# Immediate cosine constants, small temporaries in one PSUM tile, and wider row statistics in an S4D convolution with a SwiGLU block

## The chip, the cores and the metric

The kernel runs on one core of a Trainium2 chip. The metric is the time of one execution on the device, in microseconds. Its engines are named as the profile names them: PE (TensorE matmul), PEld (its weight load), DVE (VectorE), ACT (ScalarE), POOL (GpSimd) and SP (SyncE, which issues the DMAs).

## The reference

The input `x` has L = 2048 positions of D = 640 channels. The block normalises each position, modulates it by a condition, convolves each channel along the positions with a kernel made from N = 128 complex modes, and then does a gated feed-forward part of width 1728.

```python
def _A_ref(u, log_A_real, A_imag, C_real, C_imag, log_dt, D_skip):
    dt = jnp.exp(log_dt)
    A = -jnp.exp(log_A_real) + 1j * A_imag
    C = (C_real + 1j * C_imag) * dt[:, None]
    P = jnp.exp((A * dt[:, None])[:, :, None] * pos[None, None, :])
    K = 2.0 * jnp.einsum("dn,dnl->dl", C, P).real
    y = irfft(rfft(u^T, 2L) * rfft(K, 2L))[:, :, :L]^T      # causal convolution
    return y + u * D_skip
mod = (silu(c) @ w_mod).reshape(1, 6, 1, -1)                # sa, ca, ga, sb, cb, gb
h = layernorm(x) * (1 + ca) + sa
x = x + ga * _A_ref(h, ...)
h = layernorm(x) * (1 + cb) + sb
x = x + gb * ((silu(h @ w1) * (h @ w3)) @ w2)
```

(The transforms are written in shorthand here.)

## The kernel before

**Two parts.** The first part makes the condition's modulation, the row statistics of the first normalisation, the convolution kernels and the convolution. The second is the feed-forward part (FFN), a long run of matmuls. The first part is a plan of named tasks. A task has an engine, the tasks it comes after, and slots that it takes and gives back. The table `ORDER` lists all tasks by number in the order in which they are issued; `Plan.sequence` (L175) reads it. Every engine then works strictly in that order: the wrapper `InOrder` (L150) chains each instruction behind the one before it on its engine, and this is why nearly every instruction of the profile carries the line L150. From the last task on a scheduler orders the FFN.

**Generation.** The kernels K are made for five blocks of 128 channels, in eight chunks of 16 channels each, 40 chunks in all (`gen_chunk`, L523; `gen_tasks`, L1676). Per chunk POOL adds phases (`ph`) and multiplies sizes (`xx`, `yy`, `x`), ACT takes an absolute value of the phases and four sines `tr` of 128x512, two of them as sines and two as cosines (sine of pi/2 minus the phase, L559), DVE multiplies them into `xx` and `yy`, PE sums the modes by 64 small matmuls into the product `kps` of 128x256, and ACT copies `kps` into `ks`. The product has one PSUM bank to itself (tag "kg", one buffer). The cosine takes pi/2 from `hpi`, a column of 128 values in SBUF that POOL fills in `setup`.

**The first row statistics.** The positions lie in four row blocks `xs` of 128 rows by 4 by 640. For three blocks, ACT makes a sum (a Copy with an accumulator output, into `h_nm`), DVE turns the four sums of a block into minus the mean, and ACT makes the sum of squares about the mean (a Square with `h_nm` as its bias, accumulator into `h_ss`) (`h_stats`, L338). For the fourth block, DVE does both with `bn_stats` over two halves of 320 channels and `bn_aggr` into `h_mv`, and then writes its columns of `h_nm` and `h_ss` (`end`, L360). A chain of small DVE steps (`rsqrt`, L242) makes the inverse root for all 16 columns from `h_ss`; in this call two of its temporaries (`rsw`) already lie in PSUM. The normalised rows `hn` are then made by ACT and DVE. The modulation matmuls are `pm`, their copy is `m`, the rows spread from it are `prow`.

**The second statistics.** The last inverse transform leaves its results on PE row by row (`iy`), DVE adds each to the rows `x2` (x for the first, late for the second group of four) and takes statistics of the sum by `bn_stats` over 128 channels each, four of them as the first 512 channels are done and the fifth after the last 128 channels (`iyb`) are added. `bn_aggr` makes mean and variance in `mv`. The FFN does the same for two later row groups (`ln_stats`, L627).

Of the kernel before, what the change touches and what calls it, by code (L numbers as in the profile page):

```python
# [18 lines left out]
P = 128  # L19
L = 2048  # L20
D = 640
# [59 lines left out]
1399 1395 1388 1450 1396 1400 1447 1389 1397 1398 1401 1390 1452 1392 1409 1402 1465 1393 1449 1411 1410 1391 1403 1414 1412 1416  # L81
1454 1415 1413 1417 1404 1451 1418 1419 1407 1405' 1459 1408 1460 1406 1479 1422 1420 1487 1423 1480 1461 1421 1467 1475 1482 1453
# [3 lines left out]
1578 1502 1547 1548 1512 1549 1543 1579 1550 1551 1554' 1553 1580 1555' 1509 1513 1552' 1510 1556 1581 1560 1511 1582 1587 1643 1564  # L86
# [5 lines left out]
"""  # L92
# [112 lines left out]
class K:  # L205
# [18 lines left out]
    def setup(self):  # L224
        nc = self.nc
        c = self.const = self.pool("const")
        self.ident = c.tile([P, P], F32, name="ident")
        make_identity(nc, self.ident)
        self.hpi = c.tile([P, 1], F32, name="hpi")
        nc.gpsimd.memset(self.hpi, HPI)  # L230
        self.ones = c.tile([P, 1], F32, name="ones")
        nc.gpsimd.memset(self.ones, 1.0)
        self.cols = c.tile([P, 3, KT], F32, name="cols")
        c.tile([P, 32], F32, name="pad")
        d = self.dram = self.pool("dram", space=DRAM)
        self.hs = d.tile([NB, 4, 4, 32, 4, P], F32, name="hs")
        self.zd = d.tile([32, 2, 64, D], F32, name="zd")
        self.w2d = d.tile([14, P, 2, D], F32, name="w2d")
        self.xv = self.x.rearrange("(t1 q j) d -> q t1 j d", t1=32, q=4, j=NJ)
        self.ov = self.out.rearrange("(t1 q j) d -> q t1 j d", t1=32, q=4, j=NJ)  # L240

    def rsqrt(self, pool, var, n, tag, mean, scale=1.0, work=None):  # L242

        nc = self.nc
        v, w = (pool.tile([P, n], F32, name=f"rs_{x}_{tag}", tag=f"rs_{x}") for x in "vw")
        y = pool.tile([P, n], F32, name=f"rs_y_{tag}", tag="rs_y", bufs=2)
        nb = pool.tile([P, n], F32, name=f"rs_n_{tag}", tag="rs_n", bufs=2)
        t, u = work or (pool.tile([P, n], F32, name=f"rs_t_{tag}", tag="rs_t"), w)
        nc.vector.tensor_scalar(v, var, scale, EPS, op0=ALU.mult, op1=ALU.add)
        wi = w.bitcast(I32)  # L250
        nc.vector.tensor_scalar(wi, v.bitcast(I32), 1, None, op0=ALU.logical_shift_right)
        nc.vector.tensor_scalar(wi, wi, -1.0, float(0x5F3759DF), op0=ALU.mult, op1=ALU.add)
        for i in range(3):

            if work:
                nc.vector.tensor_copy(u, w)
            nc.vector.tensor_mul(t, u, w)
            nc.vector.scalar_tensor_tensor(t, t, -0.5, v, op0=ALU.mult, op1=ALU.mult)
            nc.vector.scalar_tensor_tensor(y if i == 2 else w, t, 1.5, w, op0=ALU.add, op1=ALU.mult)
        m, s = mean  # L260
        nc.vector.scalar_tensor_tensor(nb, m, s, y, op0=ALU.mult, op1=ALU.mult)
        return y, nb

    def ln_begin(self, pool, tag):
        return (pool.tile([P, 4, KT, 6], F32, name=f"st_{tag}", tag="ln_st", bufs=2),
                pool.tile([P, 4, 2], F32, name=f"mv_{tag}", tag="ln_mv", bufs=2))

    def ln_part(self, st, xs, j, c0, c1):
        for c in range(c0, c1):
            self.nc.vector.bn_stats(st[:, j, c, :], xs[:, j, c * P:(c + 1) * P])  # L270

# [29 lines left out]
    def load_c(self, e):  # L301
        nc = self.nc
        ct = e.tile([P, KT], F32, name="ct")
        nc.sync.dma_start(ct, self.c.rearrange("o (k p) -> p (o k)", p=P))
        th = e.tile([P, KT], F32, name="th")
        self.sc = self.const.tile([P, KT], F32, name="sc")

        def sc():
            nc.vector.scalar_tensor_tensor(self.sc, th, 1.0, ct, op0=ALU.add, op1=ALU.mult)
            nc.vector.tensor_scalar(self.sc, self.sc, 0.5, None, op0=ALU.mult)  # L310
        return lambda: nc.scalar.activation(th, ct, AF.Tanh, scale=0.5), sc
# [26 lines left out]
    def h_stats(self, xs, b):  # L338
# [3 lines left out]
        def sums(j):  # L342
            nc.scalar.activation(xs[:, j], xs[:, j], AF.Copy, accum_out=self.h_nm[:, 4 * b + j:4 * b + j + 1])

        def mean():
            o = slice(4 * b, 4 * b + 4)
            nc.vector.tensor_scalar(self.h_nm[:, o], self.h_nm[:, o], -1.0 / D, None, op0=ALU.mult)

# [3 lines left out]
        if b in self.W["stat_v"]:  # L352
            st = self.gp.tile([P, 4, 2, 6], F32, name=f"h_st{b}", tag="h_st", bufs=1)
            mv = self.gp.tile([P, 4, 2], F32, name=f"h_mv{b}", tag="h_mv", bufs=1)

# [167 lines left out]
    def gen_chunk(self, d0, tabs, off, E, place):  # L523
# [27 lines left out]
        def sines(i):  # L551
# [74 lines left out]

    def ln_stats(self, b, st, mv, c0):  # L627
        for j in range(4):
            self.ln_part(st, self.x2[b], j, c0, KT)
        return self.ln_end(self.fp, st, mv, f"n{b % 2}")  # L630
# [376 lines left out]
    def tail_tasks(self, border, cut):  # L1007
# [109 lines left out]
        def rows(b, rank):  # L1117
            for j in range(4 * b, 4 * b + 4):
# [40 lines left out]
        def last_stats(b):  # L1159
            for j in range(4):  # L1160
                self.ln_part(self.stats[b][0], self.x2[b], j, KT - 1, KT)
        add("izb0", "SP", 0, lambda: last_load(0), ends, -100, dma=[131072] * 4, take=[("w2", 1)])
# [7 lines left out]
        def prepare(b, rank):  # L1170
# [8 lines left out]
            add(f"lm{b}", "DVE", .68, mean, [f"isb{b}"] + [f"is{j}.{c}" for j in range(4 * b, 4 * b + 4) for c in range(2)], rank)  # L1179
            if b == 0:  # L1180
# [177 lines left out]
    def groups(self, p, tiles, X, acc, W, w2, pend):  # L1358

        for m in tiles:  # L1360
# [24 lines left out]
            if p == 0 and m in (8, 10):  # L1385
                b = m // 2 - 2
                self.stats[b % 2] = self.ln_stats(b, *self.ln_begin(self.fp, f"n{b}"), 0)
        return pend
# [95 lines left out]
    def run(self):  # L1484
# [118 lines left out]
    def param_steps(self, T, bs):  # L1603
# [23 lines left out]
             ("arc", lambda V: (A.activation(at, k, AF.Arctan), A.activation(s, at, AF.Sin),  # L1627
                                A.activation(m, at, AF.Sin, scale=-1.0, bias=self.hpi)))],
            [tt(k, k, s, ALU.mult),
# [46 lines left out]
    def gen_tasks(self, b):  # L1676
# [266 lines left out]
    def early_tasks(self, e):  # L1943
# [175 lines left out]
```

## Time and profile before

| | |
|---|---|
| time, median of three runs | 955.36 us (954.37 to 956.51) |
| the profiled execution | 954.89 us |
| its span in the profile | 953.1 us |
| PE busy | 870.5 us (91%) |
| DVE busy | 682.3 us (72%) |
| ACT busy | 551.5 us (58%) |
| POOL busy | 344.1 us (36%) |

The table's shares are means over the whole span. The views used below are: the busy time of each engine in chosen stretches, the groups of equal instructions (busy time, mean length, idle time in front of them and what ended it), the waits of one engine in a stretch, and the timeline of one engine, where each row has its start, its length, and in brackets the idle time before it and the engine and result that ended it. A row with "x4" holds four instructions of a kind in a row, and its length goes from the start of the first to the end of the last.

### The profile page before, as it was taken

What the parts mean: (1) busy time and instruction counts of PE and PEld (TensorE: products, weight loads), DVE (VectorE), ACT (ScalarE), POOL (GpSimd) and SP (SyncE); (2) the same over time, 40 slices, a digit from 0 to 9 for tenths busy, and PEclk for the clock granted to TensorE, in tenths of its full rate; (3) what the DMA queues carried; (4) which work ended last, traced back from release to release, by engine and by line L of the source; (5) the groups of instructions that cost most, each with busy time, mean ns of one, the idle gap of its engine ahead of it and who ended that gap; (6) DMA issues with size and microseconds to landing.
All of it is one profiled execution on the core that took longest, in us unless ns stands there. A gap on an engine that the chain in (4) does not pass through costs nothing.

```text
span 953.1 us, 21244 instructions
## 1 busy us (share of the span) xinstructions
PE 870.5 (91%) x8369; PEld 689.6 (72%) x8369; DVE 682.3 (72%) x1290; ACT 551.5 (58%) x1036; POOL 344.1 (36%) x376
## 2 busy tenths in 40 slices
PE   1266999999989997899999999999999999999997
PEld 1134968877878875686777778888788888888775
DVE  7988999999989878776676775657555555555412
ACT  3989999998877733644444444545444444443312
POOL 2698999999987400011111111000121212120000
PEclk9987999999999997999999999999999999999999
DMA  9974454453173578754444412375432222221374
GB/s 199 284 266 112 158 134 137 101 146 83 47 173 93 134 189 212 179 179 125 148 116 123 139 63 91 92 237 168 130 91 84 83 84 83 84 84 38 110 217 132
DMA packets 110508, 127.42 MB, mean 134 GB/s; under 512 B 10568, under 2 KB 90696, under 8 KB 109128
## 3 DMA queue, kind: packets, MB, share of 16 engines
q1 hardware_dynamic: 110120, 125.80, 46.9%
q8 instruction: 66, 1.08, 0.5%
q14 instruction: 34, 0.28, 0.1%
q10 hardware_dynamic: 288, 0.26, 0.1%
HBM read 95.89 MB, written 30.15 MB: 132 GB/s over the span
## 4 chain that ended last, share of the span: by engine, by line
PE 55%; DMA 2%; ACT 2%; DVE 2%; SPq 1%; issue 1%; DVEq 0%
PE c L150 19%; PE acc L150 18%; PE X L150 12%; PE gu L150 3%; PE iy L150 1%; DMA w2r<-in_w 1%; DMA w<-w2d 1%; PE to L150 1%; PE tp L150 1%; PE gh L150 1%; ACT oc L978 0%; PE iyb L150 0%; SPq L991 0%; DMA izb<-zd 0%; DMA zd<-zt 0%
## 5 line engine op out<-in xcount | busy, mean ns | idle before, releaser
L150 PE MATMUL acc<-ah,w 128*128 128x512 f32 x560 | 173.0, 394 | 3.0 <-DMA w<-w2d 2.3
L150 PEld LDWEIGHTS acc<-ah,w 128*128 128x128 f32 x560 | 103.7, 188 | 26.6 <-issue 2.7
L775 POOL TENSOR_TENSOR s<-wr 128x256 f32<-128x256 f32 x22 | 16.6, 753 | 277.3 <-DMA wr<-in_w 133.0
L150 PE MATMUL acc<-al,w 128*128 128x512 f32 x260 | 102.2, 393 | 0.0
L599 DVE TENSOR_TENSOR wl<-s,wh 128x256 fp32r<-128x256 f32 x92 | 39.0, 424 | 67.3 <-ACT wh L598 66.8
L598 ACT ACTIVATE wh<-s 128x256 fp32r<-128x256 f32 x92 | 37.6, 410 | 78.3 <-PE X L150 57.9
L150 POOL TENSOR_TENSOR ph<-p,p 128x1024 int32<-128x1024 int32 x40 | 79.0, 1974 | 6.4 <-ACT tr L150 4.2
L598 ACT ACTIVATE wh<-wr 128x256 fp32r<-128x256 f32 x92 | 38.4, 418 | 57.6 <-PE X L150 42.0
L776 POOL TENSOR_TENSOR s<-s,wr 128x256 f32<-128x256 f32 x22 | 16.6, 753 | 132.2 <-issue 130.9
L150 DVE TENSOR_TENSOR yy<-yy,tr 128x512 f32<-128x512 f32 (+1 forms) x60 | 56.8, 947 | 6.3 <-POOL yy L150 3.3
L150 PE MATMUL kps<-yy,xx 128*32 128x64 f32 x1920 | 38.2, 230 | 22.4 <-DVE xx L150 19.9
L150 ACT ACTIVATE tr<-ph,hpi 128x512 f32<-128x512 f32 x80 | 54.4, 689 | 6.9 <-DVE yy L150 5.9
L836 ACT ACTIVATE t<-g 128x512 f32<-128x512 f32 x44 | 27.8, 632 | 52.7 <-DVE g L800 52.7
L150 PEld LDWEIGHTS acc<-al,w 128*128 128x128 f32 x260 | 48.9, 188 | 10.8 <-DVE al L599 0.4
L805 DVE SCALAR_TENSOR_TENSOR g<-t,g 128x512 f32<-128x512 f32 x48 | 33.7, 702 | 31.2 <-ACT t L836 29.3
L150 PEld LDWEIGHTS kps<-yy,xx 128*32 128x32 f32 x1920 | 32.7, 114 | 31.1 <-issue 17.5
L150 DVE TENSOR_TENSOR xx<-tr,xx 128x512 f32<-128x512 f32 x80 | 54.3, 683 | 0.7
L150 PE MATMUL fz<-fp,wz 64*128 64x512 f32 x224 | 54.5, 607 | 0.1
L599 DVE TENSOR_TENSOR wl<-wr,wh 128x256 fp32r<-128x256 f32 x92 | 40.7, 443 | 14.8 <-ACT wh L598 14.7
L150 ACT ACTIVATE tr<-ph 128x512 f32<-128x512 int32 x80 | 46.5, 598 | 4.2 <-DVE yy L150 2.7
L150 PE MATMUL ps<-wk,xb 128*64 128x128 f32 x640 | 46.8, 294 | 1.2 <-DVE hb L150 0.4
L598 ACT ACTIVATE ah<-h 128x512 fp32r<-128x512 f32 x26 | 16.5, 633 | 53.8 <-PE acc L150 53.8
(452 smaller groups left out, 2450.7 us busy)
## 6 DMA issues: line engine op xcount, KB each, us to landing
w<-w2d SPq DMA_DIRECT2D x42, 640.0 KB, 3.9
wr<-in_w SPq DMA_DIRECT2D x50, 320.0 KB, 3.6
zd<-zt SPq DMA_DIRECT2D x40, 256.0 KB, 2.5
w2d<-w SPq DMA_DIRECT2D x14, 640.0 KB, 3.5
xs<-in_x SPq DMA_DIRECT2D x16, 320.0 KB, 10.9
hs<-hb SPq DMA_DIRECT2D x20, 256.0 KB, 2.8
xb<-hs SPq DMA_DIRECT2D x20, 256.0 KB, 5.5
iz<-zd SPq DMA_DIRECT2D x32, 160.0 KB, 4.3
```

Of the source, the lines that this page charges most:

```text
L150: self.prev = self.k.order(f(*a, **kw), self.prev)
L598: self.nc.scalar.activation(H, v, AF.Copy)
L599: eng.tensor_tensor(Lo, v, H.bitcast(F32), op=ALU.subtract)
L775: eng.tensor_tensor(s[0], u[:, 0:2], u[:, 2:4], op=ALU.add)
L776: eng.tensor_tensor(s[1], s[0], g[:, 0:2], op=ALU.subtract)
L805: V.scalar_tensor_tensor(g, th, 1.0, g, op0=ALU.add, op1=ALU.mult)
L836: tanh = lambda o, i: A.activation(o, i, AF.Tanh, scale=0.5)
```

## The change

Three edits. The order table's numbers shift, since two statistics tasks per row become one; the tasks keep their order, except that these merged tasks of the second row group stand further ahead (third place below).

1. Cosines take pi/2 as an immediate of the instruction; the column `hpi` goes.
2. A PSUM tile `small` of 128x512 stays in the bank that the product had. Its second half is `kps` of every chunk. Its first half holds the silu's temporaries (columns 0 to 12), the sums and the sums of squares of the first statistics (`h_sum`, `h_ss`, columns 16 to 47) and the fourth block's means and variances. `h_nm` stays in SBUF. `rsqrt` writes its first shift to another of its temporaries.
3. `bn_stats` of the second statistics runs over 512 and 128 channels, not five times 128.

```diff
-        self.hpi = c.tile([P, 1], F32, name="hpi")
-        nc.gpsimd.memset(self.hpi, HPI)
...
-                A.activation(t, ab[:, :, 4 - i, :], AF.Sin, scale=-SINS, bias=self.hpi)
+                A.activation(t, ab[:, :, 4 - i, :], AF.Sin, scale=-SINS, bias=HPI)
...
+        self.small = psg.tile([P, 512], F32, name="small", tag="kg", bufs=1)
...
-                kps[c] = self.psg.tile([P, 256], F32, name=f"kps{b}{c}", tag="kg", bufs=1)
+                kps[c] = self.small[:, 256:]
...
-        th = e.tile([P, KT], F32, name="th")
+        th, u = self.small[:, :KT], self.small[:, 8:8 + KT]
...
-        for x in ("h_nm", "h_ss"):
-            setattr(self, x, self.gp.tile([P, NJ], F32, name=x))
+        self.h_nm = self.gp.tile([P, NJ], F32, name="h_nm")
+        self.h_sum, self.h_ss = self.small[:, 16:32], self.small[:, 32:48]
...
-            nc.scalar.activation(xs[:, j], xs[:, j], AF.Copy, accum_out=self.h_nm[:, 4 * b + j:4 * b + j + 1])
+            nc.scalar.activation(xs[:, j], xs[:, j], AF.Copy, accum_out=self.h_sum[:, 4 * b + j:4 * b + j + 1])
...
-            nc.vector.tensor_scalar(self.h_nm[:, o], self.h_nm[:, o], -1.0 / D, None, op0=ALU.mult)
+            nc.vector.tensor_scalar(self.h_nm[:, o], self.h_sum[:, o], -1.0 / D, None, op0=ALU.mult)
...
-            mv = self.gp.tile([P, 4, 2], F32, name=f"h_mv{b}", tag="h_mv", bufs=1)
+            mv = self.small[:, 64 + 8 * b:72 + 8 * b].rearrange("p (j a) -> p j a", a=2)
...
-        nc.vector.tensor_scalar(wi, v.bitcast(I32), 1, None, op0=ALU.logical_shift_right)
-        nc.vector.tensor_scalar(wi, wi, -1.0, float(0x5F3759DF), op0=ALU.mult, op1=ALU.add)
+        ui = u.bitcast(I32)
+        nc.vector.tensor_scalar(ui, v.bitcast(I32), 1, None, op0=ALU.logical_shift_right)
+        nc.vector.tensor_scalar(wi, ui, -1.0, float(0x5F3759DF), op0=ALU.mult, op1=ALU.add)
...
-    def ln_part(self, st, xs, j, c0, c1):
-        for c in range(c0, c1):
-            self.nc.vector.bn_stats(st[:, j, c, :], xs[:, j, c * P:(c + 1) * P])
+    def ln_part(self, st, xs, j, c):
+        self.nc.vector.bn_stats(st[:, j, c, :], xs[:, j, 512 * c:min(512 * c + 512, D)])
...
-                for c in range(2):
-                    add(f"is{j}.{c}", "DVE", .4, lambda j=j, c=c: self.ln_part(self.stats[b][0], self.x2[b], j % 4, 2 * c, 2 * c + 2), [f"ia{j}"], rank + .1)
+                add(f"is{j}", "DVE", .6, lambda j=j: self.ln_part(self.stats[b][0], self.x2[b], j % 4, 0), [f"ia{j}"], rank + .1)
```

What stands where is seen best in the program's order. First ACT in the startup, where the sums (`xs` with `h_nm` as second output, Copy) and the squares (`xs` with `h_ss`) of three row blocks stand among the first sines. Before:

```order
L150 ACTIVATE tr0_0_338<-ph_0_313 128x512 [waits Pool_49]
L150 ACTIVATE xs0_185,h_nm_134<-xs0_185 128x640
L150 ACTIVATE xs1_148,h_ss_135<-xs1_148,h_nm_134 128x640 [waits DVE_49]
L150 ACTIVATE xs0_185,h_nm_134<-xs0_185 128x640
L150 ACTIVATE xs1_148,h_ss_135<-xs1_148,h_nm_134 128x640
L150 ACTIVATE xs2_176,h_ss_135<-xs2_176,h_nm_134 128x640 [waits DVE_49]
L150 ACTIVATE tr1_0_363<-ph_0_313 128x512
```

The same place after the change; `small` is the PSUM tile:

```order
L150 ACTIVATE tr0_0_334<-ph_0_309 128x512 [waits Pool_49]
L150 ACTIVATE xs0_182,small_78<-xs0_182 128x640 [waits DVE_49,Activation_49]
L150 ACTIVATE xs1_145,small_78<-xs1_145,h_nm_133 128x640 [waits Activation_49]
L150 ACTIVATE xs0_182,small_78<-xs0_182 128x640 [waits Activation_49]
L150 ACTIVATE xs1_145,small_78<-xs1_145,h_nm_133 128x640 [waits Activation_49]
L150 ACTIVATE xs2_173,small_78<-xs2_173,h_nm_133 128x640 [waits DVE_49]
L150 ACTIVATE tr1_0_359<-ph_0_309 128x512
```

The order is the same. Each statistic now waits for the one before it on ACT, and the first of these rows also waits for DVE, which reads `small` ahead of it.

Second, DVE in the startup, where the fourth block's statistics are put together (`h_st` are its partial statistics) and PE's first product follows on them. Before, and after:

```order
L150 BN_AGGR h_mv_236<-h_st_235 128x2 x2
L150 BN_AGGR h_mv_236<-h_st_235 128x2 [waits DVE_49]
L150 BN_AGGR h_mv_236<-h_st_235 128x2
L150 TENSOR_SCALAR h_nm<-h_mv_236 128x4 [waits DVE_49]
L150 TENSOR_SCALAR h_ss<-h_mv_236 128x4
L150 SCALAR_TENSOR_TENSOR yy_373<-yy_373,tr_16_456 128x16x32 [waits Activation_49,Pool_49]
```

```order
L150 BN_AGGR small<-h_st_232 128x2 [waits Activation_49]
L150 BN_AGGR small<-h_st_232 128x2 [waits DVE_49] x3
L150 TENSOR_SCALAR h_nm<-small 128x4 [waits DVE_49]
L150 TENSOR_SCALAR small<-small 128x4 [waits DVE_49]
L150 SCALAR_TENSOR_TENSOR yy_369<-yy_369,tr_16_451 128x16x32 [waits Activation_49,Pool_49]
```

Again nothing moved, and the first aggregate waits for ACT's last statistic ahead of it, the other five for the one before. PE's first product, `kps<-yy,xx` before and `small<-yy,xx` now, waited for DVE's `xx` and for POOL; now it waits for the last of these rows and for ACT as well. The next statistic on ACT waits for the end of that product.

Third, DVE at the end of the first part, where the rows of the last inverse transform (`iy`, then `iyb`) are added and their statistics taken (`st`). Before:

```order
L150 TENSOR_TENSOR x_94<-iy_5338,x_94 128x512 [waits PE_49]
L150 BN_STATS st_5020<-x_94 128x6 x2
L150 TENSOR_TENSOR late<-iy_5344,late 128x512 [waits PE_49]
L150 BN_STATS st_5020<-x_94 128x6 [waits DVE_49]
L150 BN_STATS st_5020<-x_94 128x6 x3
L150 TENSOR_TENSOR late<-iy_5357,late 128x512 [waits PE_49]
L150 TENSOR_TENSOR late<-iy_5361,late 128x512 [waits PE_49]
L150 BN_STATS st_5020<-x_94 128x6 x4
L150 TENSOR_TENSOR x_94<-iyb_5395,x_94 128x4x128 [waits PE_49]
```

After:

```order
L150 TENSOR_TENSOR x_93<-iy_5295,x_93 128x512 [waits PE_49]
L150 BN_STATS st_4976<-x_93 128x6 [waits DVE_49]
L150 TENSOR_TENSOR late<-iy_5300,late 128x512 [waits PE_49]
L150 BN_STATS st_4978<-late 128x6 [waits DVE_49]
L150 TENSOR_TENSOR late<-iy_5310,late 128x512 [waits PE_49]
L150 BN_STATS st_4978<-late 128x6 [waits DVE_49]
L150 TENSOR_TENSOR late<-iy_5315,late 128x512 [waits PE_49]
L150 BN_STATS st_4978<-late 128x6 [waits DVE_49]
L150 TENSOR_TENSOR x_93<-iyb_5343,x_93 128x4x128 [waits PE_49]
```

The statistics of the second row group (`late`), which stood behind the `iyb` addition, now stand ahead of it, one behind each addition: eight of 512 channels where sixteen of 128 were.

More of the change, by code (lines that the diff above doesn't have):

```diff
@@ L81 @@
 1399 1395 1388 1450 1396 1400 1447 1389 1397 1398 1401 1390 1452 1392 1409 1402 1465 1393 1449 1411 1410 1391 1403 1414 1412 1416
-1454 1415 1413 1417 1404 1451 1418 1419 1407 1405' 1459 1408 1460 1406 1479 1422 1420 1487 1423 1480 1461 1421 1467 1475 1482 1453
[3 rows of a table removed]
-1578 1502 1547 1548 1512 1549 1543 1579 1550 1551 1554' 1553 1580 1555' 1509 1513 1552' 1510 1556 1581 1560 1511 1582 1587 1643 1564
[5 rows of a table removed]
+1454 1415 1413 1417 1404 1451 1418 1419 1407 1405' 1459 1408 1460 1406 1477 1422 1420 1483 1423 1478 1479 1461 1421 1467 1474 1453
[3 rows of a table added]
+1542 1543 1546' 1545 1572 1547' 1501 1505 1544' 1502 1548 1573 1552 1503 1574 1579 1635 1556 1575 1598 1560 1549 1633 1580 1564 1550
[5 rows of a table added]
 """
@@ L233, in setup @@
         self.cols = c.tile([P, 3, KT], F32, name="cols")
-        c.tile([P, 32], F32, name="pad")
+        c.tile([P, 40], F32, name="pad")
         d = self.dram = self.pool("dram", space=DRAM)
@@ L264, in ln_begin @@
     def ln_begin(self, pool, tag):
-        return (pool.tile([P, 4, KT, 6], F32, name=f"st_{tag}", tag="ln_st", bufs=2),
+        return (pool.tile([P, 4, 2, 6], F32, name=f"st_{tag}", tag="ln_st", bufs=2),
                 pool.tile([P, 4, 2], F32, name=f"mv_{tag}", tag="ln_mv", bufs=2))
-    def ln_part(self, st, xs, j, c0, c1):
-        for c in range(c0, c1):
-            self.nc.vector.bn_stats(st[:, j, c, :], xs[:, j, c * P:(c + 1) * P])
+    def ln_part(self, st, xs, j, c):
+        self.nc.vector.bn_stats(st[:, j, c, :], xs[:, j, 512 * c:min(512 * c + 512, D)])
     def ln_mean(self, st, mv):
@@ L304, in load_c @@
         nc.sync.dma_start(ct, self.c.rearrange("o (k p) -> p (o k)", p=P))
-        th = e.tile([P, KT], F32, name="th")
+        th, u = self.small[:, :KT], self.small[:, 8:8 + KT]
         self.sc = self.const.tile([P, KT], F32, name="sc")
         def sc():
-            nc.vector.scalar_tensor_tensor(self.sc, th, 1.0, ct, op0=ALU.add, op1=ALU.mult)
-            nc.vector.tensor_scalar(self.sc, self.sc, 0.5, None, op0=ALU.mult)
+            nc.vector.scalar_tensor_tensor(u, th, 1.0, ct, op0=ALU.add, op1=ALU.mult)
+            nc.vector.tensor_scalar(self.sc, u, 0.5, None, op0=ALU.mult)
         return lambda: nc.scalar.activation(th, ct, AF.Tanh, scale=0.5), sc
@@ L625, in inverse_row, with ln_stats @@
         return half
-    def ln_stats(self, b, st, mv, c0):
+    def ln_stats(self, b, st, mv):
         for j in range(4):
-            self.ln_part(st, self.x2[b], j, c0, KT)
+            for c in range(2):
+                self.ln_part(st, self.x2[b], j, c)
         return self.ln_end(self.fp, st, mv, f"n{b % 2}")
@@ L1160, in last_stats @@
             for j in range(4):
-                self.ln_part(self.stats[b][0], self.x2[b], j, KT - 1, KT)
+                self.ln_part(self.stats[b][0], self.x2[b], j, 1)
         add("izb0", "SP", 0, lambda: last_load(0), ends, -100, dma=[131072] * 4, take=[("w2", 1)])
@@ L1178, in mean @@
                 ln[b], steps[0] = self.ln_steps(self.fp, self.stats[b][1], f"n{b}")
-            add(f"lm{b}", "DVE", .68, mean, [f"isb{b}"] + [f"is{j}.{c}" for j in range(4 * b, 4 * b + 4) for c in range(2)], rank)
+            add(f"lm{b}", "DVE", .68, mean, [f"isb{b}"] + [f"is{j}" for j in range(4 * b, 4 * b + 4)], rank)
             if b == 0:
@@ L1386, in groups @@
                 b = m // 2 - 2
-                self.stats[b % 2] = self.ln_stats(b, *self.ln_begin(self.fp, f"n{b}"), 0)
+                self.stats[b % 2] = self.ln_stats(b, *self.ln_begin(self.fp, f"n{b}"))
         return pend
@@ L1627, in param_steps @@
              ("arc", lambda V: (A.activation(at, k, AF.Arctan), A.activation(s, at, AF.Sin),
-                                A.activation(m, at, AF.Sin, scale=-1.0, bias=self.hpi)))],
+                                A.activation(m, at, AF.Sin, scale=-1.0, bias=HPI)))],
             [tt(k, k, s, ALU.mult),
```

16 rows, old and new, of the table ORDER are left out of this document.

## The prediction

> **What bounds the kernel now.** I read the profiled execution (954.89 us, span 953.1 us) first in stretches of time, since an average over a kernel with a generation part and a matmul part says little. Columns: busy microseconds of PE, PEld, DVE, ACT and POOL, then the granted clock.
>
> ```profile
> 60.00:80.00 20.00, 7.59 (x214) 5.14 (x217) 16.29 (x36) 17.63 (x34) 17.30 (x20) 0.83 0.49 169
> 80.00:100.00 20.00, 17.94 (x405) 13.04 (x397) 17.82 (x31) 17.96 (x30) 18.93 (x18) 0.91 0.67 169
> 100.00:150.00 50.00, 48.49 (x1000) 39.09 (x1000) 48.69 (x71) 48.67 (x89) 47.32 (x49) 1.00 0.50 136
> 150.00:200.00 50.00, 48.35 (x1020) 40.78 (x1019) 48.88 (x75) 48.76 (x86) 48.89 (x49) 1.00 0.44 114
> 200.00:250.00 50.00, 49.62 (x1026) 39.60 (x1024) 48.68 (x76) 45.47 (x77) 48.18 (x46) 1.00 0.38 99
> 250.00:300.00 50.00, 47.59 (x1020) 40.01 (x1018) 44.08 (x74) 36.77 (x63) 44.42 (x47) 0.97 0.42 105
> 300.00:350.00 50.00, 50.00 (x974) 42.01 (x970) 43.01 (x75) 32.02 (x59) 17.78 (x15) 1.00 0.65 157
> 500.00:600.00 100.00, 100.00 (x439) 77.12 (x438) 67.24 (x150) 45.36 (x94) 15.12 (x20) 1.00 0.32 99
> ```
>
> Three different regimes. Up to 80 us PE is nearly empty and the other engines hand work round in a fixed order. From 100 to 250 us four engines are each about 97% busy, so none of them is the bound alone. From 300 us, and in the whole FFN, PE is full. An edit to DVE or ACT in the FFN is therefore worth nothing; one in the startup moves everything behind it; one in the middle is worth only what the other three engines let through.
>
> **The cosines.** The cosine read a column `hpi` as its bias, the sine has none. From the costliest groups, then DVE's waits from 100 to 250 us:
>
> ```profile
> L150 ACT ACTIVATE tr<-ph,hpi 128x512 f32<-128x512 f32 x80 | 54.4, 689 | 6.9 <-DVE yy L150 5.9
> L150 ACT ACTIVATE tr<-ph 128x512 f32<-128x512 int32 x80 | 46.5, 598 | 4.2 <-DVE yy L150 2.7
> ```
>
> ```profile
> DVE x L150 <- ACT tr L150: 0.9, 2, 0.5
> DVE yy L150 <- ACT tr L150: 0.5, 1, 0.5
> ```
>
> With an immediate the cosine should take the sine's 598 ns: 80 x 0.091 = 7.3 us of ACT work goes. How much of it reaches the end? DVE, busy for 146.25 of the 150 us, waited for ACT only 0.9 + 0.5 = 1.4 us there; when ACT hands over sooner, these waits go and DVE's own work is next. I take 1.4 us off the end. The bounds are 0 (ACT's time turns into waits for DVE, which are already the cosines' releaser in the row) and the full 7.3: PE's idle time from 80 to 300 us is 2.06 + 1.51 + 1.65 + 0.38 + 2.41 = 8.0 us, so PE would allow it.
>
> **Small temporaries in one PSUM tile.** `small` is one tile in one bank, and in the built program its users wait for one another although their columns are disjoint (the listings above show it): the accumulator outputs on ACT, the aggregates on DVE, and the product of each generation chunk on PE. ACT's timeline first (start, duration, instruction, idle before):
>
> ```profile
> 31.36 0.19 ACT L150 ACTIVATION_READ_ACCUMULATOR xs<-xs 128x1 f32 x1
> 31.46 0.72 ACT L150 ACTIVATE xs<-xs 128x640 f32<-128x640 f32 x1
> ...
> 38.63 0.72 ACT L150 ACTIVATE xs<-xs 128x640 f32<-128x640 f32 x1
> ...
> 39.95 0.83 ACT L150 ACTIVATE xs<-xs,h_nm 128x640 f32<-128x640 f32 x1 [0.50 <-DVE h_nm L150]
> ...
> 42.31 0.81 ACT L150 ACTIVATE xs<-xs,h_nm 128x640 f32<-128x640 f32 x1
> ...
> 50.68 0.81 ACT L150 ACTIVATE xs<-xs,h_nm 128x640 f32<-128x640 f32 x1
> ...
> 52.53 0.81 ACT L150 ACTIVATE xs<-xs,h_nm 128x640 f32<-128x640 f32 x1
> ...
> 56.23 0.67 ACT L150 ACTIVATE tr<-ph,hpi 128x512 f32<-128x512 f32 x1
> 57.41 0.65 ACT L150 ACTIVATE m<-pm 128x384 f32<-128x384 f32 x2 [0.50 <-PE pm L150]
> ...
> 70.70 1.95 ACT L150 ACTIVATE hn<-sp,rs_n_h,rs_y_h 128x128 f32<-128x128 f32 x4 [0.67 <-ACT ph L150]
> ...
> 73.06 3.80 ACT L150 ACTIVATE hn<-sp,rs_n_h,rs_y_h 128x128 f32<-128x128 f32 x8
> ```
>
> A statistic is an ACTIVATE and a read of its accumulator; the next ACTIVATE starts at 31.46, 0.09 before that read ends (31.36 + 0.19). When it must wait for the read, the 0.09 goes, and a wait on the engine itself costs a little more: 0.02 to 0.04 in the `hn` rows, taking 0.46 us as one's length ((3.80 - 0.46) / 7 = 0.477 from start to start). That is 0.12 per adjacent pair.
>
> DVE's timeline of the same stretch:
>
> ```profile
> 38.74 0.87 DVE L150 BATCH_NORM_STATS2 h_st<-xs 128x6 f32<-128x320 f32 x2
> ...
> 41.62 0.33 DVE L150 TENSOR_SCALAR h_nm<-h_nm 128x4 f32<-128x4 f32 x1 [1.64 <-ACT xs L150]
> ...
> 50.52 0.41 DVE L150 BATCH_NORM_AGGREGATE h_mv<-h_st 128x2 f32<-128x12 f32 x4
> 50.97 0.94 DVE L150 TENSOR_SCALAR h_nm<-h_mv 128x4 f32<-128x4 f32 x1
> 51.82 1.11 DVE L150 TENSOR_SCALAR h_ss<-h_mv 128x4 f32<-128x4 f32 x1
> ...
> 66.60 0.52 DVE L150 TENSOR_SCALAR rs_v_h<-h_ss 128x16 f32<-128x16 f32 x1
> 67.16 0.17 DVE L150 TENSOR_SCALAR rs_w_h<-rs_v_h 128x16 int32<-128x16 int32 x1
> ```
>
> Then PE's, and one row of POOL's:
>
> ```profile
> 50.75 1.96 PE L150 MATMUL kps<-yy,xx 128*32 128x64 f32 x64 [7.65 <-DVE xx L150]
> 52.64 0.29 PE L150 MATMUL kps<-dsk,ident 32*32 32x4 f32 x8
> ...
> 66.23 1.16 PE L150 MATMUL kps<-x,xx 128*32 128x64 f32 x64 [1.25 <-DVE xx L150]
> ```
>
> ```profile
> 58.12 1.95 POOL L150 TENSOR_TENSOR ph<-p,p 128x1024 int32<-128x1024 int32 x1
> ```
>
> The replay, step by step:
>
> 1. The Copy at 38.63 now waits for the two `h_nm` on DVE that read `small` and end at about 40.0: +1.35. The 0.50 of waiting behind it is used up, so the first Square is at +0.9. The third `h_nm` (41.62) now waits for the Square that stands behind the sum it needs, and the Square of 42.31 waits for it: about 43.9, +1.6.
> 2. Four adjacent Squares up to 50.68 add 4 x 0.12 = 0.5, two cosines give 0.2 back: the last Square before the aggregates ends at 51.58 + 2.0 = about 53.5.
> 3. The first aggregate (50.52) now waits for that Square, and the six small DVE instructions wait each for the last. The 15 dependent ones from 67.16 to the `hn` at 70.70 take 3.54 / 15 = 0.24 each, a longer last one included; at 0.21 they end at 53.5 + 6 x 0.21 = 54.8.
> 4. PE's first product waited for DVE's `xx` only, at 50.75. It now waits for the last of these six: about 54.9, +4.1. Behind it in PE's order stand the modulation matmuls `pm`, for which ACT's `m` at 57.41 waits: +4.1.
> 5. The Square of 52.53 waits for the end of that product, 54.9 + 1.9 + 0.3 = 57.1: +4.6. ACT keeps that to 57.41, less the idle 0.50 there: +4.2.
> 6. POOL's phase at 58.12 waits for the cosine of 56.23, which ended at 56.9: 1.2 us to spare. With the cosine at +4.5 that leaves +3.2 or a little more. From there to the row statistics' inverse root POOL sets the pace.
> 7. `rs_v_h` (66.60) reads `small`, so it waits for the third product: 66.23 + 3.2 + 1.1 + 0.2 = 70.8, +4.2. Its 16 steps follow; the first may be shorter by 0.3. ACT's `hn` at 70.70 waits for the last: about +3.7.
>
> ACT is continuously occupied after that, and everything follows it in a fixed order, so **+3.7 us** goes through to the stage from 100 us on. Lower bound +1.5: the waits on ACT itself free, step 6 with twice the slack, and the short op at step 7. Upper bound +5.5: in step 3 the two rows of 0.94 and 1.11 us keep their length, 56.3 for 54.8. I take the short value, since an operand in PSUM is what the chain from 67.16 on has (`rsw`) at 0.17 us.
>
> The Trainium skill, "VectorE: DVE Perf Modes", sections "Why PSUM operands drop a tier" and "Two Vector instructions with no wait between them", has a fp32 two-port mode that uses a second SBUF read interface, shared with GpSimd, and says that an operand in PSUM excludes it; by it the two operations shrink and the sum is +3.7, without it +5.2. No row of before has one operation in both places; the nearest are these 0.94 and 0.17.
>
> The skill's "PSUM — Partial Sum Buffer", section "PSUM bank collisions raise a hardware error", asks for semaphores by bank and quadrant and not by address, which speaks against sharing this bank; by address the startup would lose nothing and the sum would be -0.5. No run here shows a collision.
>
> **Statistics over 512 and 128 channels.** This matters once, where the first part hands over to the FFN, 355 to 372 us:
>
> ```profile
> 355.79 0.69 DVE L150 TENSOR_TENSOR x<-iy,x 128x512 f32<-128x512 f32 x1 [1.68 <-PE iy L150]
> 356.51 0.49 DVE L150 BATCH_NORM_STATS2 st<-x 128x6 f32<-128x128 f32 x2
> ...
> 357.84 1.28 DVE L150 TENSOR_TENSOR x<-iy,x 128x512 f32<-128x512 f32 x2
> ...
> 363.36 0.87 DVE L150 BATCH_NORM_STATS2 st<-x 128x6 f32<-128x128 f32 x4
> 365.23 0.69 DVE L150 TENSOR_TENSOR x<-iyb,x 128x512 f32<-128x512 f32 x1 [1.00 <-PE iyb L150]
> ...
> 366.74 0.72 DVE L150 BATCH_NORM_AGGREGATE mv<-st 128x2 f32<-128x30 f32 x4
> ```
>
> One statistic of 128 channels costs 0.20 from start to start (0.49 = 0.28 + 0.20), one of 320 costs 0.40 (38.74: 0.87 = 0.475 + 0.395); a straight line gives 0.59 for 512. Before, 16 of 128 (half of the rows) stood ahead of the `iyb` addition: 3.2 us. Now 8 of 512 (all rows) stand there: 4.7 us, +1.5. Each also waits for its addition just before: 0.72 (355.79 to 356.51) for 0.60 (1.28 less 0.68), and five more of them do than before: +0.6. DVE is done at 364.23 + 2.1 = 366.4 and not 364.23, and the addition of 365.23 slides by +1.2; 1.00 of DVE's idle time is the cover that is used up. The aggregate over 12 values takes 0.41 (50.52) for 0.72: -0.3. **Net +0.9 us**, through the normalisation and the weight split to the load of the FFN's first weights, with PE waiting at its end. The 16 fewer behind it (16 x 0.20 = 3.2 us of DVE) lie beside that load, and the FFN's 24 fewer under a full PE: 0.
>
> **Sum:** 954.89 + 3.7 - 1.4 + 0.9 = **958.1 us**. The three runs before have their median at 955.36, 0.5 above the profiled one, and scatter by 1.1 either way; I leave the forecast where the sum puts it.
>
> **Rivals.**
> - *Faster: ACT bounds the middle after all.* ACT is at 97% from 100 to 200 us and POOL and DVE both wait for its sines. If each 0.09 is passed on, all 7.3 us come back: 954.89 + 3.7 + 0.9 - 7.3 = 952.2. It decides from a return of 6.5 us on. Against it: only 1.4 us of DVE's time is put down to ACT, and the cosines' own idle rows name DVE. 15%.
> - *The startup delay is absorbed.* At step 6 POOL has more slack than counted, or the aggregates were not what the first product waits for last: +1.5 in place of +3.7, 955.9, no change that could be told. 22%.
> - *Longer.* Small DVE ops stay long and the middle gives nothing back: 954.89 + 5.2 + 0.9 = 961.0. 13%.
> - *The cosine keeps its length*, for instance since the 91 ns are those of the float input against the integer one. The Square with a column takes 0.81 and the Copy without 0.72, both with float input, so I give it little: inside my forecast, 959.5. 5%.
>
> My forecast proper, 957.0 to 960.0, has 45%. Within 0.2% (1.9 us, about what a measurement of this kernel can tell from no change) means 953.5 to 957.3. Slower: 45 + 13 + 5 less 5 at the lower edge = 58%; same: 22 + 5 = 27%; faster: 15%. The range leaves out most of the faster rival and the top of the longer one: 953.5 to 961.0.
>
> **What would show it.** Right: cosines near 0.60; the first product at about 55 with a wait for a small DVE op; `hn` at 74 to 75; the aggregates after the last Square; the `iyb` addition one microsecond later behind the chunk before. Wrong: the first product before 52 us, `hn` before 72, or a stage from 100 to 300 us that is shorter by over 3 us.

## The result, and the profile after

The changed kernel takes 968.32 us, the median of four runs (966.29 to 970.22); the kernel before took 954.95 in its four. The ratio is 1.0137, with a 95% interval of 1.0112 to 1.0162. It is slower, as forecast, but by 13 us and not by 3, and 968 lies above the range. The profiled execution took 967.86 us, its span is 966.1 us.

Where do the 13 us arise? The table gives the start of one and the same instruction in the two profiles, in microseconds.

| instruction | before | after | delay |
|---|---|---|---|
| ACT, first `hn` | 70.70 | 73.91 | +3.2 |
| ACT, an `hz` copy at the end of the generation stages | 349.29 | 351.73 | +2.4 |
| ACT, first `xn` of the FFN | 370.13 | 373.75 | +3.6 |
| ACT, first `w` (waits for the load `w2r`) | 385.71 | 390.94 | +5.2 |
| DVE, an addition to `x` in the FFN | 541.04 | 548.04 | +7.0 |
| ACT, a `t` near the FFN's end | 877.08 | 889.85 | +12.8 |

The first 3.6 us, up to the first `xn`, lie in the stretches of which the prediction speaks. 1.6 come in at a load (`w2r`) behind them. The rest, 7.5 us between the table's fourth and last rows, grows through some 490 us of matmuls, where the prediction had put nothing.

**The startup** went much as replayed. ACT's timeline after (start, duration, instruction, idle time before it and what ended it):

```profile
30.99 0.15 ACT L150 ACTIVATION_READ_ACCUMULATOR xs<-xs 128x1 f32 x1
31.17 0.74 ACT L150 ACTIVATE xs<-xs 128x640 f32<-128x640 f32 x1
...
39.59 0.74 ACT L150 ACTIVATE xs<-xs 128x640 f32<-128x640 f32 x1 [0.74 <-DVE h_nm L150]
...
43.29 0.83 ACT L150 ACTIVATE xs<-xs,h_nm 128x640 f32<-128x640 f32 x1 [0.23 <-DVE h_nm L150]
...
56.60 0.83 ACT L150 ACTIVATE xs<-xs,h_nm 128x640 f32<-128x640 f32 x1 [2.91 <-PE small L150]
...
61.15 0.65 ACT L150 ACTIVATE m<-pm 128x384 f32<-128x384 f32 x2 [0.42 <-PE pm L150]
...
73.91 1.95 ACT L150 ACTIVATE hn<-sp,rs_n_h,rs_y_h 128x128 f32<-128x128 f32 x4 [1.10 <-issue]
```

DVE's, then PE's first product:

```profile
52.71 0.97 DVE L150 BATCH_NORM_AGGREGATE small<-h_st 128x2 f32<-128x12 f32 x4 [1.09 <-ACT xs L150]
53.72 0.16 DVE L150 TENSOR_SCALAR h_nm<-small 128x4 f32<-128x4 f32 x1
53.92 0.17 DVE L150 TENSOR_SCALAR small<-small 128x4 f32<-128x4 f32 x1
...
70.46 0.17 DVE L150 TENSOR_SCALAR rs_v_h<-small 128x16 f32<-128x16 f32 x1 [1.01 <-PE small L150]
```

```profile
54.23 1.96 PE L150 MATMUL small<-yy,xx 128*32 128x64 f32 x64 [11.06 <-DVE small L150]
```

These new waits of the replay are named by the profile: the Square of 56.60 by the product in the same bank, the product by the small DVE operation, that chain by ACT's last statistic, `rs_v_h` by the third product. The first product starts at 54.23, where the replay had about 54.9. The start of a statistic now lies 0.03 behind the end of the accumulator's read (30.99 + 0.15 to 31.17).

**The cosines.** The groups by form, 0 to 350 us, after:

```profile
L150 ACT ACTIVATE tr<-ph 128x512 f32<-128x512 f32 x80 | 47.2, 599 | 6.3 <-DVE yy L150 5.2 <-DVE xx L150 0.3
L150 ACT ACTIVATE tr<-ph 128x512 f32<-128x512 int32 x80 | 46.7, 599 | 4.8 <-DVE yy L150 3.2 <-DVE xx L150 0.7 <-POOL ph L150 0.5
```

The cosine has come down to the sine's length, 599 ns, and the delay from the `hn` to 349 us shrank by 0.8 us only.

**The second statistics**, DVE after:

```profile
358.27 0.69 DVE L150 TENSOR_TENSOR x<-iy,x 128x512 f32<-128x512 f32 x1 [1.68 <-PE iy L150]
359.00 0.69 DVE L150 BATCH_NORM_STATS2 st<-x 128x6 f32<-128x512 f32 x1
...
368.57 0.69 DVE L150 BATCH_NORM_STATS2 st<-late 128x6 f32<-128x512 f32 x1
369.18 0.67 DVE L150 TENSOR_TENSOR x<-iyb,x 128x512 f32<-128x512 f32 x1
...
370.68 0.41 DVE L150 BATCH_NORM_AGGREGATE mv<-st 128x2 f32<-128x12 f32 x4
```

From the first `iy` addition to the `iyb` addition it took 365.23 - 355.79 = 9.44 us before and 369.18 - 358.27 = 10.91 after: +1.47, where +1.2 was forecast, and the idle time in front of `iyb` is gone. The aggregate gives 0.31 back. Behind it stands the load that opens the FFN, in the chain that ended last, before and after:

```profile
376.79 8.89 DMA w2r<-in_w
```

```profile
380.42 10.50 DMA w2r<-in_w
```

It lands 1.6 us later against its issue. Over the profiles of all the runs below, the step from the first `xn` to the first `w` lies between 1.0 us less than before and 2.5 more, without regard to the edits: the changed kernel with its FFN in the old places shows none, the one with the moving operands back has +2.5, and the kernel before with nothing but 384 unused bytes +1.9. What sets it stays open.

**The FFN.** The stretch from 700 to 860 us (busy microseconds and number of instructions of PE, PEld, DVE, ACT, POOL; granted clock), before, and after:

```profile
700.00:860.00 160.00, 160.00 (x701) 131.34 (x700) 90.75 (x175) 69.86 (x154) 29.60 (x40) 1.00 0.27 83
```

```profile
700.00:860.00 160.00, 160.00 (x688) 128.42 (x687) 89.26 (x170) 68.34 (x150) 29.24 (x41) 1.00 0.28 84
```

PE is full in both, the clock is 1.00 in both, the matmuls are the same and stand in the same order. Yet 688 of them fit where 701 did. The chain of waits shows it at one run of 15 matmuls, before 3.43 us, after 3.50:

```profile
703.90 3.43 PE acc L150 x15
```

```profile
709.83 3.50 PE c L150 x15
713.33 3.50 PE acc L150 x15
```

Over the starts of some 2,200 pairs of neighbouring 128x512 matmuls of the FFN (those less than 300 ns apart, as a longer distance is a wait or a missing row of the trace) the mean distance in time is 229.1 ns before and 233.4 after, from its first microseconds to its last. Some 1,916 of these pairs lie between the table's fourth and last rows. They take 438.9 us before and 446.9 after: 8.0 more, which is the whole of the 7.5 us that arise there. The matmul itself became dearer, and no instruction at it had been touched.

What differs is where its operands lie. The tile of the second statistics shrank from 480 to 192 bytes in each partition, and there are two on each side of SBUF. In the program's allocation the FFN's weights moved down by 576 bytes, the moving operands (`x`, `a`) up by 576. All 2,296 pairs of operands in this FFN keep one distance modulo 512 bytes: the start of the moving operand less the start of the weights was 64, and is 192. (The column `hpi`, which went too, was made up for: an unused tile, `pad`, grew from 32 to 40 columns. Nothing made up for the smaller statistics' tile.)

### The profile page after: what moved, and what is told of

It is laid out like the page before. It is cut to its first block, busy times and chain, and to the rows that moved or that the text cites. A ratio compares the mean times of both kernels' runs of the same rounds, so it can differ in the third digit from the quotient of the medians.

```text
span 966.1 us, 21197 instructions
## 1 busy us (share of the span) xinstructions
PE 879.4 (91%) x8369; PEld 688.9 (71%) x8369; DVE 677.9 (70%) x1242; ACT 546.2 (57%) x1036; POOL 343.9 (36%) x375
## 4 chain that ended last, share of the span: by engine, by line
PE 75%; DMA 8%; DVE 7%; ACT 5%; issue 3%; SPq 2%; POOL 1%; DVEq 0%; ACTq 0%; POOLq 0%
PE c L150 19%; PE acc L150 18%; PE X L150 12%; PE ps L150 5%; PE small L150 4%; PE fz L150 4%; PE fh L150 3%; PE fk L150 3%; PE gu L150 3%; DMA xs<-in_x 2%; SPq L150 1%; PE iy L150 1%; ACT xs L150 1%; DVE hn L150 1%; DMA w2r<-in_w 1%
## 5 line engine op out<-in xcount | busy, mean ns | idle before, releaser
L150 PE MATMUL acc<-ah,w 128*128 128x512 f32 x560 | 175.3, 398 | 1.7 <-DMA w<-w2d 1.1
L150 ACT ACTIVATE tr<-ph 128x512 f32<-128x512 f32 (+1 forms) x160 | 92.7, 599 | 11.0 <-DVE yy L150 8.4
L150 PE MATMUL small<-yy,xx 128*32 128x64 f32 x1920 | 37.5, 228 | 25.1 <-DVE xx L150 11.6
L150 PEld LDWEIGHTS small<-yy,xx 128*32 128x32 f32 x1920 | 32.3, 113 | 33.8 <-issue 30.0
L150 PEld LDWEIGHTS ps<-wk,xb 128*64 128x64 f32 x640 | 42.8, 218 | 5.8 <-issue 2.7
```

Source lines behind the costliest of these rows:

```text
L150: self.prev = self.k.order(f(*a, **kw), self.prev)
```

## The experiments

**First theory (A): the places of the operands in SBUF cost the FFN its time; rival (B): the changed instructions do.** Under A the moving operand's own place may decide (A1), the weights' own place (A2), or the distance between the two (A3). Four variants of the changed kernel move the FFN's tiles and nothing else. The first gives the statistics' tile its old size:

```diff
-        return (pool.tile([P, 4, 2, 6], F32, name=f"st_{tag}", tag="ln_st", bufs=2),
+        return (pool.tile([P, 4, KT, 6], F32, name=f"st_{tag}", tag="ln_st", bufs=2)[:, :, :2, :],
```

The other three add a tile that nothing uses behind the statistics' tiles, on the right (which moves the operands `x` and `a` down), on the left (weights up, the pool `xp`) or on both sides. The first of them has 64 bytes on the right:

```diff
...
+        n = 0 if pool is self.xp else 16
+        if n and str(tag) in ("1", "n3"):
+            pool.tile([P, n], F32, name=f"fill_{tag}", tag="fill", bufs=1)
...
```

> The changed kernel, with the tile of the second statistics allocated at its old size (five slots, the first two used). The FFN's tiles then lie where they lay before the change; every instruction is the changed kernel's. Theory A (the FFN's matmuls take 233.3 ns from start to start where they took 229.1, because the smaller tile shifted their operands in SBUF by 576 bytes): 229.1 ns, about 7.5 us off 968.3, so 960 to 962. Rival B (the FFN's loss comes from the changed instructions, for instance from statistics of another length beside the matmuls): 233.3 ns and 967 to 969.

> The changed kernel, with 64 bytes of filling on the right, which shifts the moving operands of the FFN's matmuls (x, a) from 32 to 96 past a multiple of 128 bytes, as before the change; the weights stay at 96. Theory A1 (the moving operand's place decides): 229 ns, 960 to 962. A2 (the weights' place decides): 233.3 ns, 968. A3 (the distance between both decides, modulo 128): 229 or less is open, another value than 233.3. Rival B: 233.3 ns, 968.

> The changed kernel, with 64 bytes of filling on the left, which shifts the FFN's weights from 96 to 32 past a multiple of 128 bytes, as before the change; the moving operands stay at 32. A1 (the moving operand's place decides): 233.3 ns, 968. A2 (the weights' place decides): 229 ns, 960 to 962. A3 (the distance decides): the same as the run with the moving operands shifted. Rival B: 233.3 ns, 968.

> The changed kernel, with 32 bytes of filling on the left and on the right, so that both operands of the FFN's matmuls start at a multiple of 128 bytes. If a start on such a multiple saves a piece of each read: under 229 ns, 955 to 960. If the places matter only against one another: like neither, with the distance 0. Rival B: 233.3 ns, 968.

| run | us | ratio to before | matmul, start to start, ns | distance mod 512 |
|---|---|---|---|---|
| old places | 957.40 | 1.0016 (0.9999 to 1.0034) | 229.1 | 64 |
| moving operands back | 962.90 | 1.0084 (1.0062 to 1.0105) | 232.5 | 128 |
| weights back | 964.36 | 1.0082 (1.0055 to 1.0110) | 232.5 | 128 |
| both at zero | 964.25 | 1.0091 (1.0056 to 1.0126) | 232.5 | 128 |

The old places alone take 11 us off, more than the 7.5 of the forecast. Between the same `w` and `t` as in the table above they take 7.8 us off in the profiles, and 1.6 at the load. The stretch from 700 to 860 us holds 700 matmuls:

```profile
700.00:860.00 160.00, 160.00 (x700) 131.28 (x700) 90.32 (x174) 69.14 (x153) 30.27 (x41) 1.00 0.28 83
```

B is out. But A1 and A2 fell too: neither operand's own place brings 229 ns back, and a start at a multiple of 128 bytes is worth nothing by itself. The three fillings move different operands by different amounts and give the same 232.5 ns; what they share is the distance between the two operands, 128 past a multiple of 512. That is A3. It can't be the distance modulo 128, as one expectation had it, since by that the kernels before and after would be alike: 64 and 192 differ by 128.

**The distance by itself.** A kernel with matmuls alone, in the FFN's pattern, where the weights start a shift further for each group of 96:

```python
...
w = [ws[:, off + 128 * (k + 4 * l):off + 128 * (k + 4 * l) + 128] for l in range(2)]
...
for a, b in ((0, 0), (0, 1), (1, 0)):
    nc.tensor.matmul(acc, w[a], x[b], start=n == 0, stop=n == 95)
...
```

> No part of the reference is computed: 20 groups of 96 matmuls (128x512, fp32r, each with its weight load, in the FFN's pattern high-high, high-low, low-high) with nothing beside them; the output is zeros. The weights' start is moved by 0, 32, ... 480 bytes against the moving operands, whose places stay; then 0, 64, 128 and 192 again. Theory A3 (the distance of the moving operand from the weights, modulo 512 bytes, sets the time of a matmul): at the distances of 64, 128 and 192 bytes the spacing of 229, 232.5 and 233.4 ns comes back, and over all 16 distances it traces a curve with a lowest point that may lie under 229. Rival C (the loss is in collisions with reads and writes of other engines and of DMAs, whose places shift too): one spacing at all distances, between 214 and 226 ns.

PE's timeline, one row for each group from `acci` (shift 256) to `accp` (480), then `accq`, which repeats the shift 0:

```profile
186.29 21.96 PE L2122 MATMUL acci<-xs,ws 128*128 128x512 f32 x96
208.09 22.55 PE L2122 MATMUL accj<-xs,ws 128*128 128x512 f32 x96
230.48 22.56 PE L2122 MATMUL acck<-xs,ws 128*128 128x512 f32 x96
252.88 22.64 PE L2122 MATMUL accl<-xs,ws 128*128 128x512 f32 x96
275.36 22.47 PE L2122 MATMUL accm<-xs,ws 128*128 128x512 f32 x96
297.66 22.57 PE L2122 MATMUL accn<-xs,ws 128*128 128x512 f32 x96
320.07 22.15 PE L2122 MATMUL acco<-xs,ws 128*128 128x512 f32 x96
342.05 22.56 PE L2122 MATMUL accp<-xs,ws 128*128 128x512 f32 x96
364.45 21.92 PE L2122 MATMUL accq<-xs,ws 128*128 128x512 f32 x96
```

From one row's start to the next are 96 matmuls: 21.80 us for `acci`, 227 ns each. Over the last 48 neighbouring starts of each group, by distance (512 less the shift):

| distance, modulo 256 | 0 | 32 | 64 | 96 | 128 | 160 | 192 | 224 |
|---|---|---|---|---|---|---|---|---|
| first half of the shifts, ns | 226.7 | 233.3 | 228.9 | 233.3 | 233.3 | 234.3 | 233.3 | 233.3 |
| second half, ns | 226.7 | 233.3 | 228.9 | 233.3 | 232.4 | 234.2 | 233.3 | 233.3 |

With nothing beside the matmuls the three values of the FFN are there: 229 at 64, 232.4 to 233.3 at 128, 233.3 at 192. The curve repeats itself after 256 bytes, to 0.1 ns everywhere but at 128, where the two halves differ by 0.9; the shift of 128, taken a second time, gave 232.4, so that this difference isn't one of place. Rival C, other engines and DMAs, is out. And there is a better place than that of before: 0, with 226.7 ns.

**The parts, one at a time.** Each part of the change alone in the kernel before, the FFN's tiles in their old places (the third with the statistics' tile at its old size).

> The kernel before with the immediate cosines alone; the FFN's tiles stay where they were. By the prediction's step: cosines of 0.60 us, 1.4 us off the end: about 953.7. By the rival that ACT bounds the middle: 7.3 off, 948. If ACT's saved time only turns into waits: 955.

> The kernel before with the PSUM tile for small temporaries alone; the FFN's tiles stay where they were. By the prediction's step: the first product at about 55 us, rows of hn at about 74.5, 3.7 us on the end: 958.8. By the rival of an absorbed startup: 1.5, 956.6.

> The kernel before with the statistics over 512 and 128 channels and their earlier place alone, the tile of the statistics at its old size, so that the FFN's tiles stay where they were. By the prediction's step: the iyb addition 1.2 us later, 0.9 us on the end: 956.0; FFN matmuls at 229.1 ns. If a statistic of 512 channels beside the matmuls slowed them: a growing loss through the FFN, 960 and over.

| part | us | ratio to before | by the ratio, us | forecast |
|---|---|---|---|---|
| cosines | 953.82 | 0.9991 (0.9973 to 1.0009) | -0.9 (-2.6 to +0.9) | -1.4 |
| PSUM tile | 957.60 | 1.0041 (1.0025 to 1.0057) | +3.9 (+2.4 to +5.4) | +3.7 |
| statistics | 955.58 | 1.0009 (0.9995 to 1.0023) | +0.9 (-0.5 to +2.2) | +0.9 |

The PSUM tile alone, PE's first product and ACT's first `hn`:

```profile
54.99 1.96 PE L150 MATMUL small<-yy,xx 128*32 128x64 f32 x64 [12.00 <-DVE small L150]
```

```profile
74.83 1.95 ACT L150 ACTIVATE hn<-sp,rs_n_h,rs_y_h 128x128 f32<-128x128 f32 x4 [1.10 <-issue]
```

Its startup ends 4.1 us late (74.83 for 70.70), and all three of these kernels keep 229.1 ns. By its interval only the PSUM tile's cost is clear of no change; for the cosines and the statistics the middles are near the forecast, and neither is shown to be anything but zero. That the cosines' 7.3 us come back is outside. The groups by form of the kernel with the cosines alone:

```profile
L150 ACT ACTIVATE tr<-ph 128x512 f32<-128x512 f32 x80 | 47.2, 599 | 7.4 <-DVE yy L150 6.3 <-DVE xx L150 0.3
L150 ACT ACTIVATE tr<-ph 128x512 f32<-128x512 int32 x80 | 46.6, 598 | 5.2 <-DVE yy L150 3.2 <-DVE xx L150 0.7 <-DVE rs_v_h L150 0.5
```

The 7.2 us of busy time are gone, and ACT waits 12.6 us ahead of its sines and cosines where it waited 11.1, mostly for DVE's `yy`. That is 1.5 of the 7.2; where the rest went these rows don't say.

**Good and bad places without the change.** The last four runs test A3 on the kernels themselves. A filling of 64 bytes brings the kernel before from 64 to the distance 0, once with the cosines and once with nothing else; 192 bytes bring the changed kernel there; 384 bytes bring the kernel before to the changed kernel's 192. The last of these edits:

```diff
...
+        if tag == "n3":
+            pool.tile([P, 96], F32, name="fill", tag="fill", bufs=1)
...
```

> The kernel before with the immediate cosines, and 64 bytes of filling on the right, so that the moving operands of the FFN's matmuls lie a multiple of 512 bytes from the weights (64 past one before). Theory A3 (the distance sets a matmul's time): 226.7 ns from start to start where it was 229.1, 2.4 ns on some 1,830 matmuls that PE does without a break, 4.5 us; with the cosines' small share 948.5 to 950. If the curve of the matmuls alone doesn't carry over to a kernel with other engines at work: 953.5 to 954.5.

> The kernel before with nothing but the 64 bytes of filling. Theory A3: 226.7 ns, 949.5 to 950.5. If the curve doesn't carry over: 954 to 955.

> The changed kernel, all its instructions, with 192 bytes of filling on the right, distance a multiple of 512 (192 past one in the changed kernel). Theory A3: 226.7 ns where it was 233.4; 4.5 us less than with the old places (957.4), about 953. If only the very places of before are good: 960 and over.

> The kernel before, no instruction changed, with 384 bytes of filling on the right: the distance becomes the changed kernel's, 192 past a multiple of 512. Theory A3: 233.4 ns, the loss of the changed kernel without the change, 962.5 to 965. If the loss belongs to the changed instructions and the old places only hid it: 954 to 956.

| run | us | ratio to before | matmul, start to start, ns |
|---|---|---|---|
| before, distance 0 | 950.44 | 0.9949 (0.9929 to 0.9969) | 227.3 |
| before, distance 0, cosines | 951.24 | 0.9967 (0.9950 to 0.9984) | 227.4 |
| after, distance 0 | 955.41 | 1.0001 (0.9979 to 1.0024) | 227.4 |
| before, distance 192 | 964.08 | 1.0103 (1.0077 to 1.0128) | 233.3 |

The same stretch of 160 us, of the kernel before at 192, of the kernel before at 0, and of the changed kernel at 0:

```profile
700.00:860.00 160.00, 160.00 (x687) 128.90 (x687) 88.21 (x169) 68.28 (x150) 29.05 (x39) 1.00 0.28 83
```

```profile
700.00:860.00 160.00, 160.00 (x708) 132.48 (x707) 91.20 (x176) 70.17 (x156) 29.46 (x40) 1.00 0.27 83
```

```profile
700.00:860.00 160.00, 160.00 (x707) 132.48 (x707) 92.02 (x177) 70.22 (x155) 29.45 (x40) 1.00 0.28 83
```

An unused tile of 384 bytes costs the kernel before 9.8 us (7.3 to 12.2 by the interval), most of what the whole change cost. In its profile, 8.0 of them lie between the same `w` and `t` as above. 64 unused bytes make it faster by 0.5%: it is the version that beats both kernels. The cosines on top show no further gain: 951.24 lies above the forecast of 948.5 to 950, and its interval overlaps with that of the 64 bytes alone. With its FFN at the distance 0 the changed kernel is level with the kernel before, which has no such help: 192 unused bytes take the 1.4% away. Its 955.41 is above the forecast of about 953, though the matmuls came close to the forecast 226.7 ns: 227.4.

## Why the prediction was wrong

- **The failed step** is that on the statistics in the FFN, "the FFN's 24 fewer under a full PE: 0", with the sentence behind it that an edit to DVE or ACT in the FFN is worth nothing. For the instructions this holds: at the old places the FFN neither gained nor lost. But the smaller tile that belongs to the edit moved every tile laid out after it, and the matmuls of the full PE went from 229.1 to 233.4 ns. The sum had no term for that, nor a rival. The run at the old places and the unchanged kernel at 192 show the cause from both sides. In the profiles the longer matmuls are 7.5 to 8 us of the 13; by the medians the places are worth some 10 to 11, and what is over isn't located, the load's 1.6 us among it.
- **The PSUM tile**: the step was right, in its chain and in its size (+3.7 forecast, +3.2 in the profile after, which has the shorter cosines in it, and +3.9 by itself). The short value for the small DVE operations was the right choice: 0.16 and 0.17 us for 0.94 and 1.11. `rs_v_h` took 0.17 for 0.52, as assumed; `rs_n_h`, for which nothing was assumed and whose operands stay in SBUF, 0.17 for 0.48. The four aggregates took 0.97 for 0.41, dependent ones at 0.25 and not 0.21. What the long ones waited for, POOL's timeline shows (in the last section).
- **The cosines**: the direction was right, the size somewhat high, 0.8 us in the profile and 0.9 (-0.9 to 2.6) by itself for 1.4. Part of the saved time shows as longer waits of ACT for DVE's `yy`, as argued for the lower bound.
- **The statistics** at the handover: right, +1.2 us from 349 to 370 us for +0.9, and the same +1.2 in the profile of the run with the statistics alone. The wait that took the place of the 1.00 of idle time is DVE's own queue, as forecast.
- **The rivals** all concerned the sizes of these terms, and none of them happened. Together the terms forecast +3.2; the changed instructions with the old places gave +1.5 (-0.1 to +3.2).
- **The signs of being right** nearly all came (cosines of 0.60 us, the product and the aggregates, the `iyb` addition; only the `hn` was at 73.91 and not 74 to 75), and the time was wrong even so. All of them lay in the first 370 us; none was set for the FFN, whose term of 0 no sign could catch.

## What to carry to other kernels

When an edit changes a tile's size, look up what is laid out behind it, on both sides of SBUF, before costing the edit: a stage that is full on PE can pay more for moved operands than the edit itself is worth. For matmuls like these (128x512, operands declared fp32r, a weight load each), keep the distance between the moving operand and the weights at a multiple of 256 bytes. The test is the time from start to start, or that of 15 matmuls in the chain of waits; the number of matmuls in a full stretch serves too, but some of their rows can be missing from a trace. And small temporaries put into one PSUM tile share its waits: in this program, columns that don't overlap didn't help.

## What the runs showed of the hardware

- A 128x512 fp32r matmul with its weight load took from 226.7 to 234.3 ns from start to start at a granted clock of 1.00, by nothing but the distance of its two operands in a partition, with a period of 256 bytes: best at 0, second at 64 (228.9), 232.4 to 234.3 elsewhere in steps of 32. The Trainium skill, "TensorE: Matmul & The Clock Gate", section "Back-to-back issue gap", has 216 ns for a single gap at N = 512 and 131 for a stream of weight loads and matmuls; it names no type there, and has no term for the places. These runs reached neither. Why the distance matters no run here shows; one without the weight loads would tell whether they take part.
- Three small DVE operations that were long before with their operands in SBUF (0.94, 1.11 and 0.52 us) ended with a POOL operation each. POOL's timeline before:

```profile
49.94 1.94 POOL L150 TENSOR_TENSOR ph<-p,p 128x1024 int32<-128x1024 int32 x1
51.84 2.08 POOL L150 TENSOR_TENSOR x<-e,e 128x512 f32<-128x512 f32 x2
...
65.14 1.95 POOL L150 TENSOR_TENSOR ph<-p,p 128x1024 int32<-128x1024 int32 x1
```

These POOL operations end at 51.88, 52.90 (the first of the two) and 67.09, and the DVE operations each 0.03 us later, at 51.91, 52.93 and 67.12. After the change the same three, with their input in PSUM, run in 0.16 to 0.17 us while POOL is busy. The Trainium skill, "VectorE: DVE Perf Modes", section "Why PSUM operands drop a tier", says that an operand in PSUM rules out the mode that takes both SBUF read ports. It doesn't say that an operation gets shorter by that; these rows show it for three, and no run here changes POOL's work to test it.

- The granted clock has a dip between 250 and 300 us in some profiles and not in others of nearly the same program. Before, and with the cosines alone:

```profile
250.00:300.00 50.00, 47.59 (x1020) 40.01 (x1018) 44.08 (x74) 36.77 (x63) 44.42 (x47) 0.97 0.42 105
```

```profile
250.00:300.00 50.00, 48.84 (x1083) 41.22 (x1083) 47.48 (x79) 36.77 (x67) 47.33 (x47) 1.00 0.46 113
```

The second kernel is 1.2 us ahead of the first at 240 us and 4.4 us at 330. It isn't the cosines: the kernel before at the distance 192, whose instructions are those of before, has no dip either (1.00), and goes from 0.8 us behind at 265 us to 2.2 ahead at 295. Of the thirteen profiles of whole kernels here, before, after and four others have the dip (0.97); the other seven don't, and gain 1.4 to 3.2 us on before between 265 and 295 us, where those with it stay within 0.8. So a single run of this program can be some 3 us off for a reason that no edit has, and a difference of less needs several.
